# Attention scores by 32-query tiles in 64x32 parts of the array, and probabilities turned in 32x32 blocks by VectorE

## The chip, the cores and the metric

The kernel runs on one core of a Trainium2 chip. The time is device microseconds from start to end of one execution; the medians are over several runs.

## What is computed

A sparse attention over 4 batches, 8 heads, 768 positions and 64 elements a head, and a gated network behind it over the 3072 tokens, all in float32:

```
k_sum = k.reshape(B, H, nb, 32, D).max(axis=3)          # 24 pooled keys of 32 positions
v_sum = v.reshape(B, H, nb, 32, D).mean(axis=3)
scores_l = scale * q @ k^T, kept where |i - j| < 16, else -1e9
scores_s = scale * q @ k_sum^T + log(32)
a = softmax(concat(scores_l, scores_s))                 # divided by its sum + 1e-9
x = a @ concat(v, v_sum)                                # heads side by side: 3072 x 512
out = (silu(x @ w_gate) * (x @ w_val)) @ w_out          # 512 -> 1536 -> 512
```

## The kernel before

The tokens go in 6 blocks of 512 (TOK), k = 0 to 5. A block's attention is four units, one for each pair of heads u; the two heads of a pair lie on partitions 0 to 63 and 64 to 127. The network of a block runs over 12 slices j of 128 of the 1536 hidden elements: `m_gate` and `m_val` (12 matmuls each, weights and inputs split into a high and a low part, three products), silu on ScalarE, a multiplication on VectorE (`m_mul`), a split into high and low (`m_high` on ScalarE, `m_low` on GpSimd), and `m_down` (12 matmuls into the accumulators acc).

One attention unit, for blocks 1 to 5:
- `a_load_windows` (L269) brings, for each tile of 64 queries (QT), a window of 96 keys (KW = 64 + 2 x 16), so that neighbouring windows overlap; `a_keys` lets GpSimd copy the 24 pooled keys behind each window, which makes KC = 120 columns a tile.
- `a_scores` (L375) computes 8 tiles x 2 heads. A matmul has 64 elements of a head times 64 queries as its weights and 120 keys as what streams through; it takes a 64x64 quarter of the array. Float32 matmuls are two instructions each in the trace. Head 0 writes a PSUM bank of the pool psy, head 1 one of psg.
- `a_max` (L416) adds a mask and takes the maximum on VectorE, 8 instructions of 128x120; `a_half_exp` has 8 exponentials on ScalarE; `a_norm` has the reciprocal of the sums on VectorE and one GpSimd multiplication of 128x960.
- `a_turn` (L478) turns the probabilities, 8 transposes on TensorE by the identity into two PSUM banks of psy (tiles pp0 and pp1); `a_turned` (L484) copies them to the tile pt, one on VectorE and one on ScalarE.
- `a_out` (L495) multiplies pt by the values into xo, 16 matmuls (32 instructions); `a_split` and `a_rest` make a high and a low part of it for the network.

Block 0 has its own forms of some steps. Everything up to the loop (block 0, block 1's attention, the unpacking of the weights) is a list written out by hand, in which each engine's order is fixed (L709 to L712). In the loop (from L716) the network of block k runs with the attention of block k + 1 between its slices: `do(3n)` behind gate, `do(3n + 1)` behind val, `do(3n + 2)` behind down. A unit is spread over such places: `put_attention` (L722) gives each step a place relative to that of `out`; a unit comes every 9 places, which are 3 slices. The last lines (L758 to L760) bind each instruction of the loop only to the last one of the hand-written list on its engine, not to each other: within the loop a planner decides the order on each engine, by the order of emission among what its estimates show ready. One tie is explicit: a unit's scores follow the `out` of the unit before.

PSUM: psg (two banks) is shared by gate, val and head 1's scores in turn; psy (two banks) by head 0's scores, the pooled values (pv), pp and xo; psc (four) holds acc. In the loop the tiles q, kw, vw, p and pt have one buffer each.

Of the kernel before, what the change touches and what calls it, by code (L numbers as in the profile page):

```python
# [10 lines left out]
F32 = mybir.dt.float32  # L11
# [6 lines left out]
B, H, S, D = 4, 8, 768, 64  # L18
DM = H * D
DFF = 1536  # L20
BLK, WIN = 32, 16
P = 128
NP = H // 2
NB = S // BLK
QT = 64
KW = QT + 2 * WIN
KC = KW + NB
TOK = 512
NT = TOK // QT
NTP = TOK // P  # L30
# [4 lines left out]
VREST = PADS - (NV - 1) * P  # L35
WARM = (4, 3)
OWN = (0,)
QC = P // NP
ODD = NT // 2
EVEN = 1 + ODD  # L40
SCALE = 1.0 / math.sqrt(D)
# [5 lines left out]
def score_bias() -> np.ndarray:  # L47

    m = np.zeros((P, 3, KC), np.float32)
    second, r = np.divmod(np.arange(P)[:, None], QT)  # L50
    c = np.arange(KW)[None, :]
    out = np.abs(r + WIN - c) >= WIN

    for v, edge in enumerate(((c < WIN) & (second == 0), c < 0, (c >= WIN + QT) & (second == 1))):
        m[:, v, :KW] = np.where(out | edge, np.float32(-1e9 / SCALE), np.float32(0))
    m[:, :, KW:] = np.float32(math.log(BLK) / SCALE)
    return m


def parts_of(k):  # L60


    found, at = [], k * TOK
    while at < (k + 1) * TOK:
        b, pos = divmod(at, S)
        n = min(S - pos, (k + 1) * TOK - at)
        found.append((b, pos, (at - k * TOK) // QT, n // QT))
        at += n
    return found
# [65 lines left out]


@with_exitstack
def body(ctx, tc, qP, kP, vT, vP, kq, kF, qF, vE, vR, vO, wgv, wends, wo, cst_in, out):
    nc = tc.nc
    def after(x, y):  # L140

# [5 lines left out]
    cst = pool("cst", 1)  # L147
# [12 lines left out]
    def copy(e, out, in_):  # L160
        if e == "a":
            nc.scalar.copy(out, in_)  # L162
        else:
            (nc.vector if e == "d" else nc.gpsimd).tensor_copy(out, in_)
# [64 lines left out]
    KT, VT, ksum, vsum, X, U = {}, {}, {}, {}, {}, {}  # L229
    pro = None  # L230
    two = None
    banks = {"g": psg, "y": psy, "c": psc}

    def a_bank(k, u, n, which="y"):
        return banks[which].tile([P, 512], F32, tag="b", name=f"{n}_{k}_{u}")
# [31 lines left out]
        U.setdefault((0, u), {})["q"] = t[:, PADS:]  # L267

    def a_load_windows(k, u):  # L269
        kw = two.tile([P, NT, KC], F32, tag="kw", name=f"kw_{k}_{u}")  # L270
        for b, pos, i, n in parts_of(k):
            src = kP[b, u]
            nc.sync.dma_start(
                kw[:, i : i + n, :KW], bass.AP(src.tensor, src.offset + pos, [[PADS, P], [QT, n], [1, KW]])
            )
        U.setdefault((k, u), {})["kw"] = kw
# [13 lines left out]
    def a_load_values(k, u):  # L290
        vw = two.tile([KC, NT, P], F32, tag="vw", name=f"vw_{k}_{u}")
        for b, pos, i, n in parts_of(k):
# [6 lines left out]
    def a_pool_keys(u, lead=WIN):  # L299
        ks = one.tile([P, NB], F32, tag=f"ks{u}", name=f"ks_{u}")  # L300
        nc.vector.tensor_reduce(  # L301
            out=ks, in_=KT[u][:, lead : lead + S].rearrange("p (n j) -> p n j", j=BLK), axis=AX.X, op=ALU.max
        )
        ksum[u] = ks

    def a_keys(k, u):
        for b, pos, i, n in parts_of(k):
            if pos == 0:
                a_pool_keys(u, 0)
            copy(  # L310
                "p",
                U[k, u]["kw"][:, i : i + n, KW:],
                ksum[u].rearrange("p (o n) -> p o n", o=1).broadcast_to([P, n, NB]),
            )

# [59 lines left out]
    def a_scores(k, u):  # L375
        t = U[k, u]
        sc = [a_bank(k, u, f"sc{h}", "yg"[h]) for h in range(2)]

        for i in range(NT):
            c, s = divmod(i, 2)  # L380
            qs = slice(i * QT, (i + 1) * QT)
            for h in range(2):
                hs = slice(h * D, (h + 1) * D)
                nc.tensor.matmul(  # L384
                    sc[h][s * QT : (s + 1) * QT, c * KC : (c + 1) * KC], t["q"][hs, qs], t["kw"][hs, i, :],
                    start=True, stop=True,
                )
        t["sc"] = sc

    def a_near(k, u):  # L390
        t = U[k, u]
# [24 lines left out]
    def a_max(k, u, g):  # L416

        t = U[k, u]
        if g == 0:
            t["p"] = (two if k else pro).tile([P, 2 * NTP, KC], F32, tag="p", bufs=1 if k else 4, name=f"p_{k}_{u}")  # L420
            t["nm"], t["sm"], t["ri"] = (
                sml.tile([P, 2 * NTP], F32, tag=x, name=f"{x}_{k}_{u}") for x in ("nm", "sm", "ri")
            )
        for c in range(NTP):
            i = g * NTP + c
            n = (k * NTP + c) % (S // P)
            nc.vector.tensor_tensor_reduce(  # L427
                out=t["p"][:, i, :],
                in0=t["sc"][g][:, c * KC : (c + 1) * KC],
                in1=bias_sb[0 if n == 0 else 2 if n == S // P - 1 else 1],  # L430
                scale=-SCALE,
                scalar=3e38,
                op0=ALU.add,
                op1=ALU.min,
                accum_out=t["nm"][:, i : i + 1],
            )

    def a_half_exp(k, u, g):
        t = U[k, u]
        for i in range(g * NTP, (g + 1) * NTP):  # L440
            nc.scalar.activation(  # L441
                out=t["p"][:, i, :],
                in_=t["p"][:, i, :],
                func=AF.Exp,
                scale=-1.0,
                bias=t["nm"][:, i : i + 1],
                accum_out=t["sm"][:, i : i + 1],
            )
# [12 lines left out]
    def a_scale(k, u):  # L461
        p, ri = U[k, u]["p"], U[k, u]["ri"]
        if on == "a":
            for i in range(2 * NTP):
                nc.scalar.mul(p[:, i, :], p[:, i, :], ri[:, i : i + 1])
            return
        (nc.vector if on == "d" else nc.gpsimd).tensor_tensor(  # L467
            out=p,
            in0=p,
            in1=ri.rearrange("p (n o) -> p n o", o=1).broadcast_to([P, 2 * NTP, KC]),  # L470
            op=ALU.mult,
        )

# [4 lines left out]
    def a_turn(k, u, g):  # L478
        ps = U[k, u][f"pp{g}"] = a_bank(k, u, f"pp{g}", on[:1] or "y")
        zeros(ps, on[1:])  # L480
        for c in range(NTP):
            nc.tensor.transpose(ps[:KC, c * P : (c + 1) * P], U[k, u]["p"][:, g * NTP + c, :], id_sb)  # L482

    def a_turned(k, u, g):  # L484
        t = U[k, u]
        if "pt" not in t:
            t["pt"] = (two if k else pro).tile([KC, 2, TOK], F32, tag="pt", bufs=1 if k else 4, name=f"pt_{k}_{u}")
        copy(on or "da"[g], t["pt"][:, g, :], t[f"pp{g}"][:KC, :])

    def a_transpose(k, u):  # L490
        for g in range(2):
            a_turn(k, u, g)
            a_turned(k, u, g)

    def a_out(k, u):  # L495
        t = U[k, u]
# [138 lines left out]
    def make_bias():  # L635

        off = float(np.float32(-1e9 / SCALE))
        m = cst.tile([P, 2, KC], F32, name="bias")
        nc.gpsimd.memset(m[:, :, :KW], 0.0)
        nc.gpsimd.memset(m[:, :, KW:], float(np.float32(math.log(BLK) / SCALE)))  # L640
        for h in range(2):
            w = m[h * QT : (h + 1) * QT, :, :KW]
            for sign, base in ((1, -1), (-1, 2 * WIN - 1)):
                nc.gpsimd.affine_select(
                    out=w, in_=w, pattern=[[0, 2], [sign, KW]], base=base, channel_multiplier=-sign,
                    compare_op=ALU.is_ge, fill=off,
                )
        nc.gpsimd.memset(m[:QT, 0, :WIN], off)
        bias_sb.update({v: m[:, v] for v in range(2)})
# [22 lines left out]
            close_pool("dec")  # L672
            wts.append(pool("wts3", 1, reuse_waits="tile"))

    bias_sb, id_sb, mean_sb = {}, None, None
    dec = open_pool("dec", 3, side="right")
    pro = open_pool("pro")
    make_bias()
# [6 lines left out]
    for n in WARM:  # L685
# [11 lines left out]
        "w_c2": w_shift, "w_s1": w_top, "w_s2": w_rest, "w_hi": w_hi, "w_lo": w_lo, "gate": m_up_gate,  # L697
        "silu": m_silu, "val": m_up_val, "mul": m_mul, "ah": m_high, "al": m_low, "down": m_down,
        "values": a_values, "load_values": a_load_values, "keys": a_keys, "pool_values": a_pool_values,
        "exp": a_exp, "norm": a_norm, "transpose": a_transpose,  # L700
    }
    traced = nc.cur_bb.bb.instructions
    n_before = len(traced)
# [9 lines left out]
    n_before = len(traced)  # L713


    seq = [(k, j) for k in range(1, NBLK) for j in range(NJ)]  # L716
    at = {}

# [2 lines left out]

    def put_attention(k, u, place, **more):  # L722
        steps = dict(
            load=-17, load_values=-9, keys=-12, pool_values=-11, scores=-9, exp=-9, norm=-3, values=-3, transpose=-1,
            out=0, split=0, rest=0,
        )
        for n, x in (steps | more).items():
            if (n, k, u) != ("load", 2, 0):
                put(place + x, step[n], k, u)

    for k in range(2, NBLK):
        for u in range(NP):
            place = 3 * NJ * (k - 2) + 9 * u + 8
            put_attention(k, u, place, **(dict(load_values=-8, keys=-7, pool_values=-6, scores=-5, exp=-5) if place == 8 else {}))

    def do(place):
        values = None
# [68 lines left out]
```

## Time and profile before

| | |
|---|---|
| median of 3 timed runs | 694.31 us (694.05 to 694.61) |
| profiled execution, its span | 693.0 us |
| TensorE busy | 686.5 us |
| ScalarE busy | 309.4 us |
| VectorE busy | 260.7 us |
| GpSimd busy | 137.5 us |

The profiled execution has no time of its own beside its span, from its first to its last instruction; the timed runs' median lies 1.3 us above it. Engines stand in the rows as PE (TensorE, PEld its weight loads), DVE (VectorE), ACT (ScalarE), POOL (GpSimd) and SP (the queue that issues DMAs). Matmuls of one group overlap, so their durations don't add up; the distance between starts is what they take. L384 stands for the scores of blocks 1 to 5, L482 for the transposes, L509 for the product with the values, L544 for gate and val, L594 for down. The TensorE clock granted is 1.00 of full speed over the span.

### The profile page before, as it was taken

The page shows a single profiled execution, that of the slowest core. Times are in us where ns is not written, and L with a number is a line of the kernel's source. Part 1 is how long each engine was busy: PE and PEld are TensorE (multiplying, and loading weights), DVE is VectorE, ACT ScalarE, POOL GpSimd, SP SyncE. Part 2 cuts the span into 40 slices and gives each one's busy share as a digit, 9 for nine tenths or more (in the row PEclk, how much of TensorE's full clock was granted, in tenths as well). Part 3 has the DMA queues.
Part 4 walks back from the last instruction along what each step waited for, and adds up shares of the span by engine and source line. Part 5 has one row for each costly group of instructions (what it writes and reads, how often), then busy time and mean ns, then how long its engine had stood idle before and what let it go on. Part 6 is the DMA issues. An engine that isn't in the chain of part 4 may idle for free.

```text
span 693.0 us, 11431 instructions
## 1 busy us (share of the span) xinstructions
PE 686.5 (99%) x4556; PEld 558.0 (81%) x4556; DVE 260.7 (38%) x743; ACT 309.4 (45%) x745; POOL 137.5 (20%) x128
## 2 busy tenths in 40 slices
PE   8999999999999999999999999999999999999997
PEld 5688888878888888888888888888888888888886
DVE  6999999934131223232323313223122131100001
ACT  6968998945351542523515424245243242211111
POOL 3110121112221212212212122121121221111110
PEclk9999999999999999999999999999999999999999
DMA  8899275054220222311304222022121000100001
GB/s 333 322 381 330 69 229 160 24 169 130 60 61 1 61 62 83 84 43 43 107 24 145 68 62 62 3 59 62 61 61 52 10 25 0 61 1 0 1 0 61
DMA packets 52966, 61.94 MB, mean 89 GB/s; under 512 B 23184, under 2 KB 40976, under 8 KB 51376
## 3 DMA queue, kind: packets, MB, share of 16 engines
q1 hardware_dynamic: 52912, 61.20, 27.2%
q8 instruction: 36, 0.59, 0.4%
q14 instruction: 18, 0.15, 0.1%
HBM read 54.90 MB, written 6.29 MB: 88 GB/s over the span
## 4 chain that ended last, share of the span: by engine, by line
PE 97%; DVE 2%; DMA 1%; issue 0%; SPq 0%; ACT 0%; DVEq 0%; ACTq 0%
PE g L544 29%; PE acc L594 29%; PE v L544 28%; PE xo L509 4%; PE pp L482 3%; PE sc L384 3%; DMA kq<-in_kF 1%; DVE p L427 1%; PE xo L517 1%; DVE ks L301 0%; PE pv L355 0%; PE pp L618 0%; PE pv L334 0%; DVE m_g L196 0%; SPq L260 0%
## 5 line engine op out<-in xcount | busy, mean ns | idle before, releaser
L594 PE MATMUL acc<-w_o,ah 128*128 128x512 f32 x576 | 178.2, 390 | 0.0
L555 DVE TENSOR_TENSOR a<-v,a 128x512 f32<-128x512 f32 x72 | 49.7, 690 | 295.2 <-PE v L544 267.2
L544 PE MATMUL g<-xh,w_gv 128*128 128x512 f32 x480 | 160.3, 395 | 0.0
L544 PE MATMUL v<-xh,w_gv 128*128 128x512 f32 x480 | 157.9, 390 | 0.0
L158 POOL TENSOR_TENSOR al<-a,ah 128x512 fp32r<-128x512 f32 x63 | 81.9, 1300 | 328.4 <-ACT ah L162 328.4
L594 PEld LDWEIGHTS acc<-w_o,ah 128*128 128x128 f32 x576 | 108.2, 188 | 22.7
L594 PE MATMUL acc<-w_o,al 128*128 128x512 f32 x288 | 114.6, 398 | 0.0
L550 ACT ACTIVATE a<-g 128x512 f32<-128x512 f32 x72 | 43.1, 599 | 155.7 <-PE g L544 154.2
L544 PEld LDWEIGHTS g<-xh,w_gv 128*128 128x128 f32 x480 | 90.1, 188 | 21.5 <-issue 1.9
L544 PEld LDWEIGHTS v<-xh,w_gv 128*128 128x128 f32 x480 | 90.1, 188 | 18.9 <-issue 0.2
L162 ACT CAST ah<-a 128x512 fp32r<-128x512 f32 x71 | 44.0, 621 | 134.8 <-DVE a L555 134.8
L544 PE MATMUL g<-xl,w_gv 128*128 128x512 f32 x240 | 93.6, 390 | 0.0
L544 PE MATMUL v<-xl,w_gv 128*128 128x512 f32 x240 | 93.4, 389 | 0.0
L441 ACT ACTIVATE p<-p,nm 128x120 f32<-128x120 f32 x192 | 73.2, 382 | 6.1 <-DVE nm L427 5.9
L594 PEld LDWEIGHTS acc<-w_o,al 128*128 128x128 f32 x288 | 54.1, 188 | 10.9 <-issue 0.2
L544 PEld LDWEIGHTS v<-xl,w_gv 128*128 128x128 f32 x240 | 45.1, 188 | 9.3
L544 PEld LDWEIGHTS g<-xl,w_gv 128*128 128x128 f32 x240 | 45.1, 188 | 8.8
L467 POOL TENSOR_TENSOR p<-p,ri 128x960 f32<-128x960 f32 x19 | 34.1, 1796 | 71.8 <-DVE ri L459 62.8
L427 DVE CUSTOM_DVE_ANT_0 p<-sc,bias 128x120 f32<-128x120 f32 x160 | 35.9, 276 | 5.1 <-PE sc L384 3.0
L441 ACT ACTIVATION_READ_ACCUMULATOR p<-p,nm 128x1 f32 x192 | 35.8, 187 | 0.0
L162 ACT CAST xh<-xo 128x512 fp32r<-128x512 f32 x23 | 13.4, 586 | 47.0 <-PE xo L509 47.0
L544 PE MATMUL g<-xh,w_g 128*128 128x512 f32 x96 | 32.7, 401 | 0.0
(99 smaller groups left out, 677.6 us busy)
## 6 DMA issues: line engine op xcount, KB each, us to landing
raw_gv<-in_wgv SPq DMA_DIRECT2D x10, 1024.0 KB, 12.1
raw_o<-in_wo SPq DMA_DIRECT2D x12, 512.0 KB, 7.7
out<-o SPq DMA_DIRECT2D x23, 256.0 KB, 2.1
kt<-in_kP SPq DMA_DIRECT2D x12, 384.0 KB, 3.7
vt<-in_vT SPq DMA_DIRECT2D x12, 384.0 KB, 3.3
kw<-in_kP SPq DMA_DIRECT2D x12, 384.0 KB, 4.5
vw<-in_vP SPq DMA_DIRECT2D x12, 384.0 KB, 3.7
kw<-in_kP SPq DMA_DIRECT2D x16, 192.0 KB, 3.6
```

The costliest lines, as they stand in the source:

```text
L158: (nc.vector if e == "d" else nc.gpsimd).tensor_tensor(out=out, in0=a, in1=b.bitcast(F32), op=ALU.subtract)
L162: nc.scalar.copy(out, in_)
L384: nc.tensor.matmul(sc[h][s * QT : (s + 1) * QT, c * KC : (c + 1) * KC], t["q"][hs, qs], t["kw"][hs, i, :], start=True, stop=True,)
L427: nc.vector.tensor_tensor_reduce(out=t["p"][:, i, :], in0=t["sc"][g][:, c * KC : (c + 1) * KC], in1=bias_sb[0 if n == 0 else 2 if n == S / ...
L441: nc.scalar.activation(out=t["p"][:, i, :], in_=t["p"][:, i, :], func=AF.Exp, scale=-1.0, bias=t["nm"][:, i : i + 1], accum_out=t["sm"][:, ...
L467: (nc.vector if on == "d" else nc.gpsimd).tensor_tensor(out=p, in0=p, in1=ri.rearrange("p (n o) -> p n o", o=1).broadcast_to([P, 2 * NTP, ...
L482: nc.tensor.transpose(ps[:KC, c * P : (c + 1) * P], U[k, u]["p"][:, g * NTP + c, :], id_sb)
L509: nc.tensor.matmul(ps[hs, qs], vw, t["pt"][:n, h, qs], start=k not in OWN or i == 0, stop=k not in OWN)
L544: nc.tensor.matmul(ps, w[:, cs], x, start=u == 0 and n == 0, stop=u == NP - 1 and n == 2)
L550: nc.scalar.activation(out=a, in_=A.pop(("g", k, j)), func=AF.Silu)
L555: nc.vector.tensor_tensor(out=a, in0=ps, in1=a, op=ALU.mult)
L594: nc.tensor.matmul(ACC[k][i], a[:, ts], w, start=j == 0 and n == 0, stop=j == NJ - 1 and n == 2)
```

## The change

For blocks 2 to 5 (k >= SHORT = 2; 16 units), a tile has 32 queries (SQ) in place of 64. The keys of a row lie as groups of 32 window keys followed by the 24 pooled ones (SB = 56 columns), so that one tile's keys (32, pooled, the next 32: SC = 88 columns) are a contiguous stretch that overlaps the next tile's by its last 32. Each 32 keys are loaded once, in pieces of 128 bytes. The scores are 32 matmuls a unit, each on a 64x32 part of the array, with 88 columns. Maxima, exponentials and the scaling keep their number and have 88 columns a row for 120.

The probabilities are no longer turned on TensorE. VectorE turns them in 32x32 blocks, straight from p to pt: 12 instructions a unit, each on 32 partitions and 8 blocks (256 elements), in two halves (`turn0`, `turn1`). pt keeps its form (120 rows of keys a 64-query tile, with zeros where a 32-query tile has no key), so `a_out` stays as it is; the zeros are written once, ahead of the loop, into one pt that all units share. The copies of pp to pt go. The masks of the new form come from a new input, in one load ahead of the loop. The scaling (`norm`) moves from place -3 to -5, and the turns stand at -3 and -2 where the transposes stood at -1; the loop's first unit has -3, -2 and -1.

```diff
+SQ = 32
+SB = SQ + NB
+SC = SB + SQ
+NS = P // SQ
+SHORT = 2
...
+def blocks_of(k):
+    return [(b, pos, i * QT // SQ + x, n * QT // SQ) for x, (b, pos, i, n) in enumerate(parts_of(k))]
...
     def a_load_windows(k, u):
+        if k >= SHORT:
+            parts = blocks_of(k)
+            kw = two.tile([P, TOK // SQ + len(parts), SB], F32, tag="kw", name=f"kw_{k}_{u}")
+            for b, pos, i, n in parts:
+                nc.sync.dma_start(
+                    kw[:, i : i + n + 1, :SQ],
+                    kP[b, u][:, pos : pos + (n + 1) * SQ].rearrange("p (n j) -> p n j", j=SQ),
+                )
+            U.setdefault((k, u), {})["kw"] = kw
+            return
...
     def a_scores(k, u):
         t = U[k, u]
         sc = [a_bank(k, u, f"sc{h}", "yg"[h]) for h in range(2)]
+        t["sc"] = sc
+        if k >= SHORT:
+            for b, pos, at, n in blocks_of(k):
+                for x in range(n):
+                    i = at + x - (at > 0)
+                    c, s = divmod(i, NS)
+                    keys = t["kw"].rearrange("p n j -> p (n j)")[:, (at + x) * SB : (at + x) * SB + SC]
+                    for h in range(2):
+                        hs = slice(h * D, (h + 1) * D)
+                        nc.tensor.matmul(
+                            sc[h][s * SQ : (s + 1) * SQ, c * SC : (c + 1) * SC],
+                            t["q"][hs, i * SQ : (i + 1) * SQ], keys[hs], start=True, stop=True,
+                        )
+            return
...
-    def a_transpose(k, u):
-        for g in range(2):
-            a_turn(k, u, g)
-            a_turned(k, u, g)
+    def begin_short():
+
+        short["p"] = two.tile([P, 2 * NTP, SC], F32, tag="p", name="p_short")
+        pt = short["pt"] = two.tile([P, 2, TOK], F32, tag="pt", name="pt_short")
+        bias = cst.tile([P, 3, SC], F32, tag="bias", name="bias_short")
+        nc.sync.dma_start(bias, bias_in)
+        for v in range(3):
+            bias_sb[v, "short"] = bias[:, v]
+        groups = pt.rearrange("p h (x y z) -> p (h x) y z", y=2, z=SQ)
+        for y in range(2):
+            at = slice(2 * SQ * (1 - y), 2 * SQ * (1 - y) + SQ)
+            nc.gpsimd.memset(groups[at, :, y], 0.0)
+
+    def a_turn_short(k, u, half):
+
+        t = U[k, u]
+        t["pt"] = short["pt"]
+        to = t["pt"].rearrange("p h (c x) -> p (h c) x", x=P)
+        for s in range(2 * half, 2 * half + 2):
+            for r, at in ((s % 2, 0), (3, SQ), (s % 2 + 1, SB)):
+                nc.vector.transpose(
+                    out=to[r * SQ : (r + 1) * SQ, :, s * SQ : (s + 1) * SQ],
+                    in_=t["p"][s * SQ : (s + 1) * SQ, :, at : at + SQ],
+                )
...
+    begin_short()
     seq = [(k, j) for k in range(1, NBLK) for j in range(NJ)]
...
         steps = dict(
-            load=-17, load_values=-9, keys=-12, pool_values=-11, scores=-9, exp=-9, norm=-3, values=-3, transpose=-1,
-            out=0, split=0, rest=0,
+            load=-17, load_values=-9, keys=-12, pool_values=-11, scores=-9, exp=-9, norm=-5, values=-3, turn0=-3,
+            turn1=-2, out=0, split=0, rest=0,
         )
...
-            put_attention(k, u, place, **(dict(load_values=-8, keys=-7, pool_values=-6, scores=-5, exp=-5) if place == 8 else {}))
+            put_attention(k, u, place, **(dict(load_values=-8, keys=-7, pool_values=-6, scores=-5, exp=-5, norm=-3, turn0=-2, turn1=-1) if place == 8 else {}))
```

`a_max`, `a_half_exp`, `a_scale` and `a_keys` take the new widths for k >= 2, and the tile of the masks shares its buffer with that of blocks 0 and 1 (tag "bias").

## Rows read from the trace of the kernel before

**Rows 1.** The page: busy us (share of the span) xinstructions of each engine.
```profile
PE 686.5 (99%) x4556; PEld 558.0 (81%) x4556; DVE 260.7 (38%) x743; ACT 309.4 (45%) x745; POOL 137.5 (20%) x128
```

**Rows 2.** The page: chain that ended last, share of the span by line.
```profile
PE g L544 29%; PE acc L594 29%; PE v L544 28%; PE xo L509 4%; PE pp L482 3%; PE sc L384 3%; DMA kq<-in_kF 1%; DVE p L427 1%; PE xo L517 1%; DVE ks L301 0%; PE pv L355 0%; PE pp L618 0%; PE pv L334 0%; DVE m_g L196 0%; SPq L260 0%
```

**Rows 3.** Timeline of TensorE around one unit: start us, us, engine, line, operation.
```profile
304.63 1.03 PE L482 MATMUL pp<-consts,p 128*120 128x128 f32 x8
...
307.82 0.61 PE L594 MATMUL acc<-w_o,ah 128*128 128x512 f32 x2
308.37 1.15 PE L509 MATMUL xo<-pt,vw 120*64 120x64 f32 x32
309.45 1.05 PE L384 MATMUL sc<-kw,q 64*64 64x120 f32 x32
310.43 0.50 PE L544 MATMUL g<-xh,w_gv 128*128 128x512 f32 x1
...
316.01 0.39 PE L594 MATMUL acc<-w_o,al 128*128 128x512 f32 x1
...
318.27 0.62 PE L594 MATMUL acc<-w_o,ah 128*128 128x512 f32 x2
318.73 0.39 PE L544 MATMUL g<-xh,w_gv 128*128 128x512 f32 x1
...
321.45 0.39 PE L544 MATMUL v<-xh,w_gv 128*128 128x512 f32 x1
...
337.28 1.05 PE L384 MATMUL sc<-kw,q 64*64 64x120 f32 x32
```

**Rows 4.** TensorE's groups by line and form: xcount, busy us, mean ns.
```profile
L482 PE MATMUL pp<-consts,p 128*120 128x128 f32 x192 | 25.6, 273 | 0.0
```

**Rows 5.** Timeline of TensorE in narrow windows: small matmuls, by part and columns.
```profile
310.01 0.38 PE L384 MATMUL sc<-kw,q 64*64 64x120 f32 x8
...
310.21 0.28 PE L384 MATMUL sc<-kw,q 64*64 64x120 f32 x4
...
23.37 0.40 PE L355 MATMUL pv<-vrows 128*32 128x128 f32 x8
...
23.48 0.29 PE L355 MATMUL pv<-vrows 128*32 128x128 f32 x4
...
12.14 0.61 PE L411 MATMUL sc<-ks,kq 64*64 64x24 f32 x32
12.68 2.21 PE L618 MATMUL pp<-warm 128*128 128x512 f32 x6
```

**Rows 6.** VectorE's groups by line and form: xcount, busy us, mean ns, idle before.
```profile
L555 DVE TENSOR_TENSOR a<-v,a 128x512 f32<-128x512 f32 x72 | 49.7, 690 | 295.2 <-PE v L544 267.2 <-ACT a L550 22.5 <-PE pp L482 4.8
...
L158 DVE TENSOR_TENSOR w_gv<-m_gv,w_gv 128x1024 fp32r<-128x1024 f32 x9 | 10.9, 1213 | 0.0
```

**Rows 7.** Timeline of VectorE between the unit's maxima and the next unit.
```profile
314.84 0.20 DVE L459 RECIPROCAL ri<-sm 128x8 f32<-128x8 f32 x1
316.55 0.69 DVE L555 TENSOR_TENSOR a<-v,a 128x512 f32<-128x512 f32 x1 [1.50 <-ACT a L550]
324.44 0.69 DVE L555 TENSOR_TENSOR a<-v,a 128x512 f32<-128x512 f32 x1 [7.20 <-PE v L544]
327.20 0.95 DVE L319 TENSOR_REDUCE vr<-vt 128x24 f32<-128x768 f32 x1 [2.07 <-PE pv L334]
328.18 0.69 DVE L164 COPY vw<-vs 24x1024 f32<-24x1024 f32 x1
332.74 0.69 DVE L555 TENSOR_TENSOR a<-v,a 128x512 f32<-128x512 f32 x1 [3.87 <-PE v L544]
```

**Rows 8.** Timeline of GpSimd in the same unit.
```profile
315.19 1.79 POOL L467 TENSOR_TENSOR p<-p,ri 128x960 f32<-128x960 f32 x1 [4.22 <-DVE ri L459]
```

**Rows 9.** The page: DMA issues, KB each, median us to landing.
```profile
kw<-in_kP SPq DMA_DIRECT2D x16, 192.0 KB, 3.6
```

**Rows 10.** Timeline of the DMA-issuing queue in the same unit.
```profile
311.00 0.38 SPq L273 DMA_DIRECT2D kw<-in_kP  x1
```

More of the change, by code (lines that the diff above doesn't have):

```diff
@@ L27 @@
 KC = KW + NB
+SQ = 32
+SB = SQ + NB
+SC = SB + SQ
+NS = P // SQ
+assert SQ == 2 * WIN
 TOK = 512
@@ L57, in score_bias, with short_bias @@
     return m
+def short_bias() -> np.ndarray:
+    m = np.zeros((P, 3, SC), np.float32)
+    group, r = np.divmod(np.arange(P)[:, None], SQ)
+    c = np.arange(2 * SQ)[None, :]
+    out = np.abs(r + WIN - c) >= WIN
+    for v, edge in enumerate(((c < WIN) & (group == 0), c < 0, (c >= WIN + SQ) & (group == NS - 1))):
+        near = np.where(out | edge, np.float32(-1e9 / SCALE), np.float32(0))
+        m[:, v, :SQ], m[:, v, SB:] = near[:, :SQ], near[:, SQ:]
+    m[:, :, SQ:SB] = np.float32(math.log(BLK) / SCALE)
+    return m
+def blocks_of(k):
+    return [(b, pos, i * QT // SQ + x, n * QT // SQ) for x, (b, pos, i, n) in enumerate(parts_of(k))]
 def parts_of(k):
@@ L137, in body @@
 @with_exitstack
-def body(ctx, tc, qP, kP, vT, vP, kq, kF, qF, vE, vR, vO, wgv, wends, wo, cst_in, out):
+def body(ctx, tc, qP, kP, vT, vP, kq, kF, qF, vE, vR, vO, wgv, wends, wo, cst_in, bias_in, out):
     nc = tc.nc
@@ L306, in a_keys @@
     def a_keys(k, u):
-        for b, pos, i, n in parts_of(k):
+        for b, pos, i, n in parts_of(k) if k < SHORT else blocks_of(k):
             if pos == 0:
                 a_pool_keys(u, 0)
+            kw = U[k, u]["kw"]
             copy(
                 "p",
-                U[k, u]["kw"][:, i : i + n, KW:],
+                kw[:, i : i + n, KW:] if k < SHORT else kw[:, i : i + n, SQ:],
                 ksum[u].rearrange("p (o n) -> p o n", o=1).broadcast_to([P, n, NB]),
@@ L387, in a_scores @@
                 )
-        t["sc"] = sc
     def a_near(k, u):
@@ L418, in a_max @@
         t = U[k, u]
+        if g == 0 and k >= SHORT:
+            t["p"] = short["p"]
+        elif g == 0:
+            t["p"] = (two if k else pro).tile([P, 2 * NTP, KC], F32, tag="p", bufs=1 if k else 4, name=f"p_{k}_{u}")
         if g == 0:
-            t["p"] = (two if k else pro).tile([P, 2 * NTP, KC], F32, tag="p", bufs=1 if k else 4, name=f"p_{k}_{u}")
             t["nm"], t["sm"], t["ri"] = (
@@ L426, in a_max @@
             n = (k * NTP + c) % (S // P)
+            kc = KC if k < SHORT else SC
+            v = 0 if n == 0 else 2 if n == S // P - 1 else 1
             nc.vector.tensor_tensor_reduce(
-                out=t["p"][:, i, :],
-                in0=t["sc"][g][:, c * KC : (c + 1) * KC],
-                in1=bias_sb[0 if n == 0 else 2 if n == S // P - 1 else 1],
+                out=t["p"][:, i, :kc],
+                in0=t["sc"][g][:, c * kc : (c + 1) * kc],
+                in1=bias_sb[v if k < SHORT else (v, "short")],
                 scale=-SCALE,
@@ L439, in a_half_exp @@
         t = U[k, u]
+        kc = KC if k < SHORT else SC
         for i in range(g * NTP, (g + 1) * NTP):
             nc.scalar.activation(
-                out=t["p"][:, i, :],
-                in_=t["p"][:, i, :],
+                out=t["p"][:, i, :kc],
+                in_=t["p"][:, i, :kc],
                 func=AF.Exp,
@@ L469, in a_scale @@
             in0=p,
-            in1=ri.rearrange("p (n o) -> p n o", o=1).broadcast_to([P, 2 * NTP, KC]),
+            in1=ri.rearrange("p (n o) -> p n o", o=1).broadcast_to([P, 2 * NTP, p.shape[2]]),
             op=ALU.mult,
@@ L637, in make_bias @@
         off = float(np.float32(-1e9 / SCALE))
-        m = cst.tile([P, 2, KC], F32, name="bias")
+        m = cst.tile([P, 2, KC], F32, tag="bias", name="bias")
         nc.gpsimd.memset(m[:, :, :KW], 0.0)
@@ L673, in next_room @@
             wts.append(pool("wts3", 1, reuse_waits="tile"))
-    bias_sb, id_sb, mean_sb = {}, None, None
+    bias_sb, id_sb, mean_sb, short = {}, None, None, {}
     dec = open_pool("dec", 3, side="right")
@@ L699, in body @@
         "values": a_values, "load_values": a_load_values, "keys": a_keys, "pool_values": a_pool_values,
-        "exp": a_exp, "norm": a_norm, "transpose": a_transpose,
+        "exp": a_exp, "norm": a_norm,
+        "turn0": lambda k, u: a_turn_short(k, u, 0), "turn1": lambda k, u: a_turn_short(k, u, 1),
     }
@@ L793 @@
         "consts": np.concatenate([score_bias()[:, 2], np.eye(P, dtype=np.float32)], axis=1),
+        "bias": short_bias(),
     }
```

## The prediction

> **What bounds the kernel now.** I read the busy shares first: TensorE works 99% of the 693.0 us span, ScalarE 45%, VectorE 38%, GpSimd 20% [rows 1]. The chain that ended last says the same by line: the three streams of the network behind the attention (g, v, acc) carry 86% of the span, and of the attention xo has 4%, the turning of the probabilities (pp, L482) 3%, and the scores (sc, L384) 3% [rows 2]. So a microsecond that leaves TensorE's queue leaves the time, as long as no other engine comes late; what an edit costs there is read from starts, not from durations, because matmuls overlap.
>
> The attention of blocks 2 to 5 is 16 units (4 blocks, 4 pairs of heads) strewn through the network's stream. One unit, in TensorE's order of time [rows 3]: pp starts at 304.63, the twelve acc matmuls follow it, xo starts at 308.37, sc at 309.45, g goes on at 310.43; the next unit's sc starts at 337.28, 27.83 us after this one's. TensorE has no idle row between them.
>
> **TensorE: the turning goes.** A unit has 8 transposes (192 in the trace [rows 4], of which 64 belong to blocks 0 and 1 and stay). What they cost is the stretch from pp's start to xo's start, 308.37 - 304.63 = 3.74 us, less the same twelve acc matmuls where no pp precedes them, 318.73 - 316.01 = 2.72 us. Of the 1.02 us left, a part is the step from acc into xo's smaller parts, which stays: xo starts 0.55 us behind the last two acc matmuls (307.82), g 0.46 us behind the same two (318.27), so 0.09 us [rows 3]. The removal is worth 0.93 us a unit, 16 x 0.93 = **14.9 us**.
>
> **TensorE: the scores in 64x32 parts.** Before, a unit's scores are 32 instructions (16 matmuls, two passes each) on four parts of 64x64, so 8 on each part, and the block lasts 310.43 - 309.45 = 0.98 us [rows 3]. The four parts start almost together, and the next four a step later: two steps lie between 310.01 and 310.21, so 0.10 us for 120 columns; with 128 columns, on four parts 32 wide, the step is 23.48 - 23.37 = 0.11 us [rows 5]. The step goes by the columns that stream through, some 0.83 ns each. Eight steps are 0.80 to 0.82 us; 0.16 to 0.18 us is entry and exit. After, there are 64 instructions of 88 columns on eight parts, again 8 on each. If all eight parts run side by side, a step is 88/120 of 0.10 us, 0.075 us, and the block is 0.18 + 8 x 0.075 = 0.78 us: 0.20 us less, 16 x 0.20 = **3.2 us**. The trace has no block with eight parts. The nearest rows bound it: four parts of either kind do run side by side, 64x64 and 128x32 [rows 5]; the low end is that eight do too. The high end is that only four do: 16 steps, 0.18 + 1.20 = 1.38 us, 0.40 us more than now, a loss of 6.4 us. I take the low end, since both ways of halving the array, by rows and by columns, are seen to work, and the change combines them.
>
> **VectorE: twelve turns a unit are added, a copy is removed.** Each turn moves 32 partitions x 256 elements. No such instruction is in the trace; the nearest are its fp32 instructions with two inputs: 690 ns for 512 elements, 1213 ns for 1024, so 523 ns for 512 elements and some 167 ns fixed [rows 6]. 256 elements then take 0.43 us, 12 of them 5.2 us a unit, without overlap. A lower price needs no figure, since 0.43 will prove hidden. The high end is that each of the eight 32x32 blocks in an instruction is paid as an instruction of its own: one of 8 elements takes 0.20 us [rows 7], so 1.6 us a turn, 19.2 us a unit. I take 0.43, nearest in size and type. It is hidden if the turns end before xo needs them. The sums' reciprocal ends at about 315.04, GpSimd scales the probabilities from 315.19 for 1.79 us (with 704 columns for 960 some 1.3, so to about 316.5) [rows 7, 8], and xo is due at about 335.1 (336.2 less the pp that has gone; 27.83 us behind 308.37). In those 18.6 us VectorE has three multiplications of 0.69 and two pieces of 0.95 and 0.69, 3.7 us [rows 7]. 14.9 us are free for 5.2; the high end doesn't fit. Between the multiplications at 316.55 and 324.44 alone lie 7.2 us. So **0 us**, and the end for the range is the third rival's. Behind a turn that waits for GpSimd's scaling stand those multiplications, which free the bank that the next v writes.
>
> The Trainium skill speaks against this edit: the page "VectorE: DVE Perf Modes", section "The three transpose paths", would turn a whole tile on TensorE, since VectorE turns only 32x32 blocks. The rows decide by who has time: here it is VectorE that idles [rows 1, 7]. By that rule the kernel would keep its pp and the 14.9 us.
>
> **The rest has one answer.** ScalarE and VectorE lose a copy of the turned tile each and work on 88 columns for 120; the eight instructions of maxima and of exponentials stay. GpSimd's scaling shrinks by a quarter; its copy of the pooled keys doubles in columns, and is hidden likewise, with the next scores an iteration away at the least. The window keys come in pieces of 128 bytes in place of 384, with twice as many pieces; the load is issued at 311.00 and needed at 337.28, and now lands in 3.6 us [rows 3, 9, 10]; at three times that, 15 us of the 26 would still be left. The extra bias load and two memsets on GpSimd come once, ahead of the loop, and their first use is behind the first gate at the earliest; uncovered, the load costs about the 3.6 us of a load of this size once [rows 9].
>
> **The sum.** 14.9 + 3.2 = 18.1 us. Against the profile's span: 693.0 - 18.1 = 674.9. The median of the timed runs is 1.3 us above that span, so **676.2 us**.
>
> **Rivals.**
> First, the eight parts don't all run at once: the loss of 6.4 us takes the place of the gain, 694.3 - 14.9 + 6.4 = 685.8 us. For it: no row shows eight. Against it: the two rows of four. Chance 0.07.
> Second, instructions have a least spacing, whatever their part, and 64 instead of 32 of them make the block longer. The shortest in the trace are 32 instructions of 24 columns in 12.68 - 12.14 = 0.54 us, 17 ns each [rows 5]. 64 at 17 ns are 1.09 us, 0.11 more than now: 694.3 - 14.9 + 1.8 = 681.2 us. Against it: the starts within one step lie closer than that (four in the row at 310.21, all but together), and 64-column weights may set the 17 ns, which halve here. Chance 0.08. The Trainium skill's page "TensorE: Matmul & The Clock Gate", section "Part 1: The HAM clock gate", states a least start-to-start of about 25 ns; by it, as an estimate, the block would be 1.6 us and the time near 690. The 17 ns of the trace already lie below it.
> Third, and slower: the turn is so slow that xo waits for it. It begins to cost at 14.9 / 12 = 1.24 us a turn; each 0.1 us above is 1.2 us a unit, 19 us in all, so from 1.34 us on the gain is eaten. At the high end of 1.6 us: 19.2 - 14.9 = 4.3 us a unit, 694.3 - 18.1 + 68.8 = 745.0 us. For it: turning is unseen here, and moves data between partitions, on a quarter of the lanes. Against it: it needs 1.34 us for 256 elements, where 1024 take 1.21 [rows 6]. Chance 0.06.
> Fourth, the order on VectorE, which the planner fixes in the loop: were all twelve turns put ahead of the multiplication at 316.55 (they wait for GpSimd until 316.5), it would end at 316.5 + 5.2 + 0.7 = 322.4, while the next v, in the same bank, starts at 321.45 [rows 3, 7]: 0.95 us a unit, 694.3 - 18.1 + 15.2 = 691.4 us. Up to nine turns ahead of it cost nothing. Chance 0.05.
>
> **How the numbers follow.** Forecast 676.2 with 0.74, its own range 673 to 680 (the low end if the 0.18 us of entry and exit of the scores goes too: 16 x 0.18 = 2.9; the high end takes in that the scores stay as long as now, 679.4). The rivals have 0.07, 0.08, 0.06 and 0.05. To leave out no more than 2 in 10 the range reaches over the first two rivals: 673 to 686. Faster by over 0.2% (1.4 us; about what a measurement of this kernel can tell from no change): the forecast, the first, second and fourth rival, 0.92 with something taken off for an unseen wait of 1 us a unit. Within 0.2%: 0.02. Slower: the third, 0.06.
>
> **What would show it.** In the profile after: pp gone from the loop (64 transposes left), acc following v at once, 2.72 us long; from sc to g 0.78 us (1.38 by the first rival, 1.1 by the second); units 26.7 us apart; turns of 0.43 us on VectorE, and no idle row on TensorE released by VectorE. I am wrong if TensorE idles ahead of xo or v, or if the sc block is longer than 0.98 us.

## The result and the profile after

The changed kernel takes 678.74 us (median of four runs, 678.02 to 679.62) against 694.37 us: a ratio of 0.9773, 95% interval 0.9759 to 0.9787. In the comparison with the experiments the same kernel took 678.45 us (678.35 to 678.96) beside 694.41. The forecast was 676.2 us, range 673 to 686. One execution each of two experiments (the scores alone, the long pieces) ran at a granted clock of 0.56 and took over 1100 us; those two are left out of the medians below.

The page of the kernel after, busy time of the engines and the chain that ended last (they answer to [rows 1, 2]):

```profile
PE 670.1 (99%) x4940; PEld 543.5 (80%) x4940; DVE 331.3 (49%) x919; ACT 298.1 (44%) x729; POOL 134.4 (20%) x130
...
PE g L619 30%; PE acc L669 29%; PE v L619 29%; PE xo L584 4%; PE sc L423 2%; DMA kq<-in_kF 1%; PE pp L537 1%; DVE p L481 1%; PE sc L434 1%; PE xo L592 1%; DVE ks L336 0%; PE pv L391 0%; PE pp L693 0%; PE pv L370 0%; DVE m_g L221 0%
```

TensorE is still the bound, at 99% of a shorter span (676.2 us). VectorE has taken on 70.6 us and stands at 49%. In the chain, pp has shrunk from 3% to 1% (blocks 0 and 1); the new scores (L423) have 2% and those of block 1, in the old form (L434), 1%, where all of them together had 3%.

TensorE's timeline after, two stretches of the loop (start us, us, engine, line, operation; answers to [rows 3]):

```profile
191.81 0.39 PE L669 MATMUL acc<-w_o,al 128*128 128x512 f32 x1
...
194.07 0.61 PE L669 MATMUL acc<-w_o,ah 128*128 128x512 f32 x2
194.62 1.15 PE L584 MATMUL xo<-pt_short,vw 120*64 120x64 f32 x32
195.70 0.96 PE L423 MATMUL sc<-kw,q 64*32 64x88 f32 x64
196.59 0.50 PE L619 MATMUL g<-xh,w_gv 128*128 128x512 f32 x1
...
301.90 1.15 PE L584 MATMUL xo<-pt_short,vw 120*64 120x64 f32 x32
302.99 0.96 PE L423 MATMUL sc<-kw,q 64*32 64x88 f32 x64
...
328.73 1.15 PE L584 MATMUL xo<-pt_short,vw 120*64 120x64 f32 x32
```

No pp stands in front of acc any more: from acc's start to xo's start are 194.62 - 191.81 = 2.81 us, where it was 3.74 with pp; the difference, 0.93, is the forecast's figure to the hundredth. xo comes 0.55 us behind the last two acc matmuls, as before. The scores last 196.59 - 195.70 = 0.89 us, 0.09 less than before and not 0.20 less. The unit between the xo at 301.90 and that at 328.73 is 26.83 us long; the same unit was 27.83 us in [rows 3], from one start of the scores to the next. So 1.00 us a unit, some 16 us in all, of the span's 16.8. (From the last xo of block 1 to that of block 5 are 445.62 us before and 429.42 after, 16.2 less over the 16 units.)

The forms of the scores, the transposes left, and the turns (xcount, busy us, mean ns, idle before and its releaser):

```profile
L423 PE MATMUL sc<-kw,q 64*32 64x88 f32 x1024 | 15.3, 242 | 0.0
L537 PE MATMUL pp<-consts,p 128*120 128x128 f32 x64 | 9.1, 275 | 0.0
L565 DVE STREAM_TRANSPOSE pt_short<-p_short 32x256 f32<-32x256 f32 x192 | 83.8, 436 | 25.9 <-POOL p_short L522 23.2
```

A turn takes 436 ns on average, where the forecast took 430 from two other instructions. VectorE's timeline in the unit whose xo is due at 328.73 (answers to [rows 7]), and in the loop's first unit its pooling of keys and its turns (last two lines),

```profile
309.91 1.33 DVE L565 STREAM_TRANSPOSE pt_short<-p_short 32x256 f32<-32x256 f32 x3 [1.54 <-POOL p_short L522]
311.27 0.69 DVE L630 TENSOR_TENSOR a<-v,a 128x512 f32<-128x512 f32 x1
312.00 4.04 DVE L565 STREAM_TRANSPOSE pt_short<-p_short 32x256 f32<-32x256 f32 x9
...
160.84 0.95 DVE L336 TENSOR_REDUCE ks<-kt 128x24 f32<-128x768 f32 x1 [2.45 <-DMA kt<-in_kP]
161.71 5.39 DVE L565 STREAM_TRANSPOSE pt_short<-p_short 32x256 f32<-32x256 f32 x12
```

and in that first unit GpSimd's scaling and TensorE's xo:

```profile
158.53 1.36 POOL L522 TENSOR_TENSOR p_short<-p_short,ri 128x704 f32<-128x704 f32 x1 [3.98 <-ACT ah L187]
...
167.73 1.15 PE L584 MATMUL xo<-pt_short,vw 120*64 120x64 f32 x32
```

The typical unit's turns end at 316.0, 12.7 us ahead of xo. In the first unit they end at 167.10, 0.63 us ahead of it: there the cover is nearly used up. A part of it went to a load. In the typical unit the first turn starts where GpSimd's scaling ends; here the scaling ends at 159.89, but VectorE's next instruction is the pooling of keys for a later unit, which waits 2.45 us for its load, and the turns behind it start only at 161.71, 1.8 us later.

### The profile page after: what moved, and what is told of

Read it like the earlier page. It is cut to its first block, busy times and chain, and to the rows that moved or that the text cites. A ratio compares the mean times of both kernels' runs of the same rounds, so it can differ in the third digit from the quotient of the medians.

```text
span 676.2 us, 12388 instructions
## 1 busy us (share of the span) xinstructions
PE 670.1 (99%) x4940; PEld 543.5 (80%) x4940; DVE 331.3 (49%) x919; ACT 298.1 (44%) x729; POOL 134.4 (20%) x130
## 2 busy tenths in 40 slices
DMA packets 72058, 60.36 MB, mean 89 GB/s; under 512 B 42144, under 2 KB 60064, under 8 KB 70464
## 4 chain that ended last, share of the span: by engine, by line
PE 97%; DVE 2%; DMA 1%; issue 0%; SPq 0%; ACT 0%; DVEq 0%; ACTq 0%
PE g L619 30%; PE acc L669 29%; PE v L619 29%; PE xo L584 4%; PE sc L423 2%; DMA kq<-in_kF 1%; PE pp L537 1%; DVE p L481 1%; PE sc L434 1%; PE xo L592 1%; DVE ks L336 0%; PE pv L391 0%; PE pp L693 0%; PE pv L370 0%; DVE m_g L221 0%
## 5 line engine op out<-in xcount | busy, mean ns | idle before, releaser
L669 PE MATMUL acc<-w_o,al 128*128 128x512 f32 x288 | 113.0, 392 | 0.0
L565 DVE STREAM_TRANSPOSE pt_short<-p_short 32x256 f32<-32x256 f32 x192 | 83.8, 436 | 25.9 <-POOL p_short L522 23.2
L496 ACT ACTIVATE p_short<-p_short,nm 128x88 f32<-128x88 f32 x128 | 45.3, 355 | 0.2
L522 POOL TENSOR_TENSOR p_short<-p_short,ri 128x704 f32<-128x704 f32 x16 | 21.8, 1364 | 57.5 <-DVE ri L514 53.6
L619 PE MATMUL v<-xh,w_v 128*128 128x512 f32 x96 | 31.9, 393 | 0.0
```

What stands on the lines that cost most here:

```text
L496: nc.scalar.activation(out=t["p"][:, i, :kc], in_=t["p"][:, i, :kc], func=AF.Exp, scale=-1.0, bias=t["nm"][:, i : i + 1], accum_out=t["sm" ...
L522: (nc.vector if on == "d" else nc.gpsimd).tensor_tensor(out=p, in0=p, in1=ri.rearrange("p (n o) -> p n o", o=1).broadcast_to([P, 2 * NTP, ...
L565: nc.vector.transpose(out=to[r * SQ : (r + 1) * SQ, :, s * SQ : (s + 1) * SQ], in_=t["p"][s * SQ : (s + 1) * SQ, :, at : at + SQ],)
L619: nc.tensor.matmul(ps, w[:, cs], x, start=u == 0 and n == 0, stop=u == NP - 1 and n == 2)
L669: nc.tensor.matmul(ACC[k][i], a[:, ts], w, start=j == 0 and n == 0, stop=j == NJ - 1 and n == 2)
```

## The experiments

Theory: the two parts of the change add up on TensorE, the turning is hidden on VectorE, and the scores gained less than forecast because of something within their block. The rivals: the scores gained what was forecast and another effect of the change (turns, small transfers, places) takes some 2 us back; and, within the block, that certain columns of the banks are slow.

### The changed kernel again

> The changed kernel once more, beside the kernels of this row on one chip. Ledger theory: 678.0 to 679.5 us, and from the start of the scores to the next g 0.89 us.

678.45 us, span of its profile 676.7 us. The next three kernels ran beside this one. Those after them ran in two further comparisons, beside the kernel before at 694.52 and 694.53 us in place of 694.41, and without the changed kernel; a difference of some tenths from 678.45 us says nothing there.

### The turning alone

```diff
     def a_load_windows(k, u):
-        if k >= SHORT:
+        if k >= NEVER:
...
     def a_scores(k, u):
...
-        if k >= SHORT:
+        if k >= NEVER:
...
-            for r, at in ((s % 2, 0), (3, SQ), (s % 2 + 1, SB)):
+            for r, at in ((s % 2, (s % 2) * SQ), (3, KW), (s % 2 + 1, (s % 2 + 1) * SQ)):
```

> Only the turning is moved to VectorE (12 turns of 32x256 a unit); the scores stay as before, 64x64 parts, 120 columns, 0.98 us a unit. Theory (the two parts add, the turning is worth 0.92 us of TensorE's time a unit, the scores 0.09): 694.4 - 16 x 0.92 = 679.7 us, about 1.5 us above the changed kernel. Rival (the scores are worth the forecast 0.20 us a unit, and something else takes 1.7 us back in the changed kernel): 682 us, 3.2 above it.

680.34 us (679.44 to 681.23), 14.1 us below the kernel before and 1.9 above the changed one. TensorE's timeline of this kernel:

```profile
194.46 1.15 PE L584 MATMUL xo<-pt_short,vw 120*64 120x64 f32 x32
195.54 1.05 PE L435 MATMUL sc<-kw,q 64*64 64x120 f32 x32
196.52 0.50 PE L619 MATMUL g<-xh,w_gv 128*128 128x512 f32 x1
```

The old scores' 0.98 us (195.54 to 196.52) stand beside the new turning. 1.9 us is nearer to the theory's 1.5 than to the rival's 3.2, but the runs of this kernel spread over 1.8 us, so the time alone does not decide. The trace does: a unit (from the xo at 302.17 to that at 329.08) is 26.91 us long, 0.08 more than in the changed kernel and not 0.20. The turning carries most of the change.

### The scores alone

```diff
-            nc.tensor.transpose(ps[:KC, c * P : (c + 1) * P], U[k, u]["p"][:, g * NTP + c, :], id_sb)
+            m = KC if k < SHORT else SC
+            nc.tensor.transpose(ps[:m, c * P : (c + 1) * P], U[k, u]["p"][:, g * NTP + c, :], id_sb)
...
-        copy(on or "da"[g], t["pt"][:, g, :], t[f"pp{g}"][:KC, :])
+        copy(on or "da"[g], t["pt"][:m, g, :], t[f"pp{g}"][:m, :])
...
-        "turn0": lambda k, u: a_turn_short(k, u, 0), "turn1": lambda k, u: a_turn_short(k, u, 1),
+        "transpose": a_transpose,
```

> Only the scores are made by 32-query tiles in 64x32 parts; the probabilities are turned by TensorE as before (8 transposes of 88 columns and two copies a unit; the rows are not sorted into place for the next product, so that the output is another one). Theory: 694.4 - 16 x 0.09 = 692.9 us, the scores' block 0.89 us. Rival (0.20 us a unit): 691.2 us, block 0.78 us.

693.13 us, 1.3 us below the kernel before (ratio 0.9981, interval 0.9972 to 0.9991): the theory's 1.5, not the rival's 3.2. Its timeline:

```profile
192.99 1.03 PE L538 MATMUL pp<-consts,p_short 128*88 128x128 f32 x8
193.78 0.48 PE L675 MATMUL acc<-w_o,al 128*128 128x512 f32 x1
...
197.79 0.96 PE L423 MATMUL sc<-kw,q 64*32 64x88 f32 x64
198.67 0.50 PE L625 MATMUL g<-xh,w_gv 128*128 128x512 f32 x1
```

The block is 0.88 us here too, with the turning on TensorE. So the loss against the forecast lies within the block of the scores. Alone, the two parts give 14.1 and 1.3 us, 15.4 together; the change gave 16.0 in the same comparison, within the runs' spread of the sum.

### Inside the scores' block: split in two

First the block as the changed kernel has it. Each line is the timeline from 195.69 to 195.95, 196.00, 196.05, 196.10, 196.20, 196.30 and 196.43; xcount is how many of the block's 64 instructions have begun by then:

```profile
195.70 0.46 PE L423 MATMUL sc<-kw,q 64*32 64x88 f32 x24
195.70 0.53 PE L423 MATMUL sc<-kw,q 64*32 64x88 f32 x32
195.70 0.56 PE L423 MATMUL sc<-kw,q 64*32 64x88 f32 x33
195.70 0.65 PE L423 MATMUL sc<-kw,q 64*32 64x88 f32 x35
195.70 0.75 PE L423 MATMUL sc<-kw,q 64*32 64x88 f32 x44
195.70 0.83 PE L423 MATMUL sc<-kw,q 64*32 64x88 f32 x54
195.70 0.96 PE L423 MATMUL sc<-kw,q 64*32 64x88 f32 x64
```

32 have begun after 0.30 us: four steps of eight instructions, eight parts at once, as forecast. The other 32 take 0.43 us: from 196.00 to 196.10 three begin, then 9, 10 and 10 in the next stretches of 0.10 to 0.13 us. A step of 0.076 us for eight (9.5 ns each) isn't kept up: only the 33rd still comes in step, and the 31 behind it follow 12.7 ns apart on average (not the 17 ns that the split's expectation gives). The break stands at the same place in all 16 units, whether VectorE works during the block or is idle in it (the block at 276.16). Does the position in the block decide, or the columns? The split kernel puts the first 32 in front of xo and the last 32, on the second half of each bank's columns, behind it:

```diff
+            if f is a_out and split:
+                a_scores(*next(x[1:] for x in steps if x[0] is a_scores), halves=(0,))
...
+            if f is a_scores and split:
+                f(*a, halves=(1,))
```

> The 64 score instructions of a unit are split: the first 32 in front of xo, the last 32 behind it. In the changed kernel the first four steps of the scores follow at 0.076 us and the later ones more slowly, with instructions about 17 ns apart. Theory (instructions held ready in TensorE's queue go at once, those behind them come only every 17 ns; xo's 32 instructions take longer than that each and let the queue fill again): all eight steps at 0.076 us. Rival (the last two of the four column groups of a bank, or something else that runs at that time, slows the last four steps): the second half slow as before. Time: each half has an entry and an exit of its own, about 0.25 us together; the second half gains 0.13: 680 to 681 us, no gain.

The second half's timeline, from 196.28 to 196.36, 196.45, 196.52 and 196.60:

```profile
196.29 0.31 PE L426 MATMUL sc<-kw,q 64*32 64x88 f32 x8
196.29 0.38 PE L426 MATMUL sc<-kw,q 64*32 64x88 f32 x16
196.29 0.46 PE L426 MATMUL sc<-kw,q 64*32 64x88 f32 x24
196.29 0.54 PE L426 MATMUL sc<-kw,q 64*32 64x88 f32 x32
```

The same instructions on the same columns that were slow behind the first 32 now begin eight by eight, and all 32 within 0.32 us. ScalarE and VectorE work beside this half too. The columns are not the cause; the position is: 32 small instructions go at once, those right behind them don't. That they wait for TensorE's instruction supply, which xo (32 instructions in 1.08 us) lets catch up, is the reading that fits; it is not shown, since no row shows the supply and no run had a block of a third length. The Trainium skill's page "TensorE: Matmul & The Clock Gate", table at its head, gives TensorE a queue of 64 instructions. As an estimate from that figure, 32 matmuls with their 32 weight loads would fill it; the trace agrees to within one pair, since 33 matmuls come in step.

The time is 678.91 us (678.45 to 680.14): no gain, since each half has its own entry and exit, though less of a loss than the 680 to 681 us expected. The timeline shows 0.47 us from the first half's start to xo and 0.46 from the second half's to g, 0.93 for 0.89 in one block, so the second entry and exit cost 0.04 us more than the faster second half gains:

```profile
194.74 0.53 PE L426 MATMUL sc<-kw,q 64*32 64x88 f32 x32
195.21 1.15 PE L587 MATMUL xo<-pt_short,vw 120*64 120x64 f32 x32
196.29 0.54 PE L426 MATMUL sc<-kw,q 64*32 64x88 f32 x32
196.75 0.50 PE L622 MATMUL g<-xh,w_gv 128*128 128x512 f32 x1
```

### How much turning is hidden

```diff
-            for r, at in ((s % 2, 0), (3, SQ), (s % 2 + 1, SB)):
+            for r, at in ((s % 2, 0), (3, SQ), (s % 2 + 1, SB)) * 2:
```

> The changed kernel with each turn made twice: 24 instead of 12 a unit, 10.5 us of VectorE. Theory (the turns are hidden in the forecast's 14.9 us of free time between the scaling and xo): 678.5 us, as the changed kernel, within 0.7 us. Rival (the turns cost a little through the waits of v or through shared ports, and that is a part of the 2 us by which the forecast was too low): 680 us or more.

686.21 us, some 7.7 above the changed kernel: the theory's 678.5 us is missed. That looks like the rival, but the trace puts it in one place. TensorE's timeline in the first unit:

```profile
173.96 1.76 PE L584 MATMUL xo<-pt_short,vw 120*64 120x64 f32 x28 [3.67 <-DVE pt_short L565]
```

and the window behind it (its us; busy time of PE, PEld, DVE, ACT and POOL; PEclk, the granted clock; DMA share, GB/s):

```profile
175.00:180.00 5.00, 5.00 (x53) 4.05 (x50) 2.92 (x11) 4.17 (x18) 0.50 (x1) 0.50 0.53 144
```

The first unit's xo waits 3.67 us for the turns, and in these 5 us behind the wait the granted clock is 0.50, 1.2 GHz for 2.4, so that the matmuls there take about twice as long. It is the only wait for the turns in the run. The same with three times the turns:

> Each turn made three times, 36 a unit, 36 x 0.436 = 15.7 us of VectorE where the forecast counts 14.9 us free. Theory: now it shows, by (15.7 - 14.9) x 16 = 13 us or somewhat more, 690 to 697 us, with TensorE waiting for VectorE in front of xo. Rival (the free time is longer, since the scaling may start earlier or xo's place may slip behind other matmuls): below 682 us.

698.91 us, above the theory's 690 to 697, with the first unit's wait in it too. So the first unit was taken out, with all others doubled, then tripled:

```diff
-            for r, at in ((s % 2, 0), (3, SQ), (s % 2 + 1, SB)):
+            for r, at in ((s % 2, 0), (3, SQ), (s % 2 + 1, SB)) * (1 if (k, u) == (SHORT, 0) else 2):
```

> Each turn made twice in all units but the loop's first. In the run with all turns doubled the whole loss of 7.7 us lies in the first unit: TensorE waits 3.7 us in front of its xo, and the granted clock is 0.50 in the 5 us behind that; the 14 distances between later units are those of the changed kernel. Theory (24 turns are hidden in 15 of 16 units): 678.5 us within 0.7. Rival (the doubled turns cost something in every unit): above 680 us.

678.41 us, the changed kernel's time. 24 turns, 10.5 us of VectorE a unit, are hidden in 15 of 16 units; the loss of the doubled run was the first unit's alone.

> Each turn made three times in all units but the loop's first, 15.7 us of VectorE a unit. Theory (some 14.9 us are free, so 0.8 us a unit is not hidden): 678.5 + 15 x 0.8 = 690 us, with TensorE waiting in front of xo or v. Rival (VectorE's own total decides, 15.7 + 6.7 of 26.8 us, and all of it stays hidden): 679 us.

690.5 us, as forecast from the 14.9 us of free time. TensorE's waits in that run (what waited for what: us in total, times, longest):

```profile
PE xo L584 <- DVE pt_short L565: 3.2, 5, 1.3
PE v L619 <- DVE nm L481: 3.0, 1, 3.0
```

The cover ends between 24 and 36 turns. The agreement with 690 is luck, though: the loss isn't 0.8 us in each unit. Half of it lies in one, between the xo at 277.02 and that at 309.80, which is 32.78 us long for 26.8. These lines are VectorE's, the DMA queue's and TensorE's there; the last one is a stretch as above:

```profile
278.21 0.95 DVE L355 TENSOR_REDUCE vr<-vt 128x24 f32<-128x768 f32 x1
...
279.19 0.34 SPq L264 DMA_DIRECT2D kt<-in_kP  x1
...
283.06 0.95 DVE L336 TENSOR_REDUCE ks<-kt 128x24 f32<-128x768 f32 x1 [3.30 <-DMA kt<-in_kP]
...
286.11 0.47 PE L619 MATMUL v<-xh,w_gv 128*128 128x512 f32 x1 [3.00 <-DVE nm L481]
...
287.40:290.80 3.40, 3.40 (x10) 2.64 (x9) 1.40 (x5) 2.21 (x4) 1.36 (x1) 0.50 1.03 195
```

The turns delay VectorE's pooling of values (vr), for whose end, at 279.16, the DMA queue has waited 15.1 us with a load of keys. The load is issued right behind it, VectorE stands idle for 3.30 us before it pools those keys, the maxima (nm) come behind that, and v waits 3.00 us for the bank that they free. In the stretch of the last line the granted clock is 0.50. So VectorE's free time ran out, and the largest single loss came through its order, by a load that it waits for, and not through a late turn.

### Small transfers and places

```diff
-                nc.sync.dma_start(
-                    kw[:, i : i + n + 1, :SQ],
-                    kP[b, u][:, pos : pos + (n + 1) * SQ].rearrange("p (n j) -> p n j", j=SQ),
-                )
+                flat = kw.rearrange("p n j -> p (n j)")
+                m = (n + 1) * SB // (2 if n > 8 else 1)
+                for x in range(i * SB, (i + n + 1) * SB, m):
+                    nc.sync.dma_start(flat[:, x : x + m], kP[b, u][:, :m])
```

> The window keys come in one or two long pieces per partition instead of 16 or 17 of 128 bytes (476 KB or 504 KB a unit instead of 272 KB; the keys lie elsewhere, so that the output is another one). Theory: the small pieces are hidden, 678.5 us. Rival (the 72,058 packets for 52,966 cost time in the transfers of other data): some 0.5 to 1 us less.

679.3 us, not less than the changed kernel, although the packets fall from 72,058 to 41,018. Their number costs nothing here; this run moves more bytes, though (63.75 MB for 60.36):

```profile
DMA packets 41018, 63.75 MB, mean 94 GB/s; under 512 B 7008, under 2 KB 29024, under 8 KB 39424
```

```diff
-            load=-17, load_values=-9, keys=-12, pool_values=-11, scores=-9, exp=-9, norm=-5, values=-3, turn0=-3,
-            turn1=-2, out=0, split=0, rest=0,
+            load=-17, load_values=-9, keys=-12, pool_values=-11, scores=-9, exp=-9, norm=-3, values=-3, turn0=-2,
+            turn1=-1, out=0, split=0, rest=0,
```

> The places only: the scaling back at -3, the turns at -2 and -1 for all units. Theory (the planner puts VectorE's and GpSimd's instructions by readiness, and their places matter only where two are ready): 678.5 us within 0.7. Rival (turns at later places end too late for xo): a wait in front of xo, up to 1 us a unit, 685 to 694 us.

678.71 us: the places decide nothing here. (The loop's first unit kept places of its own.)

## Why the prediction was right, step by step

The mechanism held: TensorE is the bound, what left it left the time, and VectorE's new work is hidden. The forecast was 2.5 us too fast, within its range; one of its terms, the scores, was mis-sized.

- **The turning** was put at 0.93 us a unit. The trace shows 0.93 between the starts, and the kernel with the turning alone 14.1 us for the 14.9 forecast.
- **The scores** are the term that was mis-sized: 0.20 us a unit forecast, 0.09 measured, 1.4 us for 3.2. The step that failed is the block of 0.18 + 8 x 0.075 = 0.78 us, with all eight steps at the low end. Half of it was right, and the bound of only four parts at a time (the first rival) is refuted: eight parts run side by side at 0.076 us for 32 instructions. The rest of the block keeps a spacing, as the second rival had it for the whole block, but 12.7 ns and not its 17: the 0.89 us lie between the forecast's 0.78 and that rival's 1.09. The forecast's sum weighed the columns and parts; how fast instructions follow each other it had as a rival only, at 0.08. [rows 5] show no block of more than 32 instructions with a step that short, so the trace before had no row on which to see it.
- **VectorE** at 0 us was right, with 436 ns a turn for 430. The 14.9 us of free time are bracketed: 24 turns a unit (10.5 us) cost nothing outside the first unit, 36 (15.7 us) cost 12 us, half of that through one late load. But they were read from one unit in the middle of the loop. The first unit, whose steps are set closer together and whose turns stand behind a wait for a load, has 0.63 us to spare. As an estimate from that, xo would be late there not from 1.24 us a turn on, as the third rival has it, but from 0.50 (5.39 + 0.63 us over 12 turns), though in one unit of 16. The twelve turns took 5.39 us there, 0.45 each; that this lies just below was luck, since the forecast did not look at that unit.
- **The order on VectorE**, the fourth rival, came halfway: three turns stand in front of the multiplication at 311.27, nine behind it, and none costs anything.
- **Around the span**: the profiled run took 678.02 us with a span of 676.2, 1.8 us around it, where the forecast took 1.3 from the median before and the span. That is 0.5 us; and the profiled run was the fastest of its four, 0.7 below their median. With 1.8 us from the scores and 0.1 from the turning (16.2 us over the units less the scores' 1.4, for 14.9), less the 0.6 us of the span's gain that lie outside the units, these make up the 2.5 us.
- The small pieces of the window keys and the places were put at nothing, and cost nothing.

## What to carry to other kernels

Where TensorE is the bound and VectorE has idle stretches, turning 32x32 blocks on VectorE moves the whole cost of a transpose off the path, if the consumer can take the blocks where they fall; look for the unit with the least time between producer and consumer, not the typical one, and for loads that the engine waits for ahead of the new work, before calling it hidden. Splitting small float32 matmuls into more, smaller parts gains only as long as the instructions keep up: four times 64x64 against eight times 64x32 was worth a tenth of the block, and its second half ran more slowly than its first, by the reading above at the pace at which instructions arrive.

## What the runs showed of the hardware

Eight 64x32 parts of the array do run side by side: a step of 88 columns takes 0.076 us on eight parts, where 120 columns took 0.10 on four [rows 5]. Behind the first 32 such instructions of a block, the other 32 took 0.43 us in place of 0.30. After a wait of 3.67 us, TensorE's granted clock was 0.50 in the 5 us shown, so that the wait cost about twice its length (7.7 us in all); after one of 3.00 us it was 0.50 from 287.40 to 290.80. A VectorE turn of 32 partitions x 256 float32 takes 436 ns.
